# One PSUM pool of single banks, block sums on VectorE, and a new written order, in a memory-attention kernel with a spatial gate

## The chip, the cores and the metric

The kernel runs on one core of a Trainium2 chip. Times are device microseconds of one execution; lower is better. Runs of the same kernel are compared by their median. The profile is that of one execution, by the hardware profiler.

## The reference

Eight batches (B), eight heads (H), 576 positions (S), head dimension 64, 32 memory slots, inner width 1024.

```python
a   = softmax(phi over positions)                  # per batch and head
k_m = einsum('bhsm,bhsd->bhmd', a, k)              # memories: 32 x 64 per head
v_m = einsum('bhsm,bhsd->bhmd', a, v)
attn = softmax(q @ k_m.T / 8) ; x = heads joined of attn @ v_m   # (b, 576, 512)
h = relu(x @ w_in) ; u, v = h[..., :512], h[..., 512:]
v_n = (v - mean(v)) / sqrt(var(v) + 1e-6)          # over the 512 columns
v_s = einsum('ts,bsd->btd', w_spatial, v_n) + b_spatial[:, None]
out = (u * v_s) @ w_out
```

## The kernel before, in words

Everything is float32. Where precision asks for it an operand is split into a high part (rounded to `fp32r`) and a low part (the rest, by a subtraction), and a product is three matmuls: high by high, high by low, low by high. So most results on TensorE are groups of 3, 6 or 12 matmuls, and each operand costs one copy on ScalarE (`...h`) and one subtraction, mostly on VectorE (`...l`).

One batch goes through these Python generators; the letter is their name in the written order.

- `P` `memory_weights` (line 351): loads `phi`, takes its maximum over positions and the exponential; the sums over positions, `es`, run on VectorE for batches 0 to 2 and on POOL for the others (`over_rows`, line 340). Its scratch tile `half` shares the tag `o`, with two buffers, with the output tile `o` of line 962.
- `K` `memories` (389): loads `k` and `v` in two parts into one buffer, tag `kv`, and multiplies by the weights: the `kvm` matmuls (412), 80 for the first part and 64 for the second. The same tag `kv` holds `vraw`, the gate's values, for batches over 0; so a load waits until the batch before has read `vraw` for the last time (line 803), the second part waits for the first part's matmuls, and the next `vraw` for the second part's.
- `Q` `queries`, `S` `scores` (611): transposes, scores on TensorE, softmax on VectorE and ScalarE, then `ah` and `al`.
- `M` `products` (675): the memories' values times `w_in`, in a two-bank tile `mp`, split into `mh` and `ml`.
- `V` `gate` (703): for five tiles of positions (the fifth of 64 rows), v of the inner layer into one bank `pv`, ReLU on ScalarE into `vraw` (767), mean and variance by two VectorE instructions (770, 771), three small POOL instructions on 128x1 columns (773 to 777), and the normalisation on ScalarE (782). Batch 0 takes the statistics another way (754 to 765): ReLU with an accumulated sum, two small POOL instructions for the mean, a Square on ScalarE with the negative mean as bias and an accumulated sum.
- `A` `blend` (792): the spatial product of 576 by 576 is done as seven block products in place of eight. For it `vraw` is combined by four additions (809) and split into `vh` (801) and `vl` (803), seven each.
- `U` `units` (824): u for one of four column tiles, 12 matmuls into the two banks of `pu`, one ReLU of 576 columns on ScalarE (844).
- `G` `spatial` (849): the seven block products for one of two column pairs, 50 matmuls of 288 columns into two two-bank tiles: `pa` holds `c11` and `p6`, `pb` holds `c12` and `c21`. `c11`, `c12` and `c21` are used twice: a first product is read, and a second is then added to it in PSUM. ScalarE copies `c11` to `p1` (895), `c21` to `p7` (899), `c12` to `p5` (911); VectorE adds `p6` to `p1` (903); POOL adds `p7` and `p1` to `p5` (913, 915); the gated results are products into `u` (907 on VectorE; 917, 925, 929 on POOL) and are split into `gh` and `gl`.
- `O` `project` (945): 12 matmuls per tile of 128 positions into one bank `po`, a copy to `o` (963) and the store. The fifth tile is done once for two batches.

For the weights there are `D` and `E`/`L` (loading and decoding `w_in`), `X` (`w_out`), `W`, `T`, `B` and `Y` (the spatial weights), and `Z` (idle matmuls).

PSUM has eight banks. Before, four are a pool of single banks (`bank`, line 107) and four a pool of two tiles of two banks (`banks`, line 110), which `mp`, `pu`, `pa`, `pb` and the transposes of the spatial weights take.

The order is written out by hand. In the strings `START`, `PLAN` and `END` a letter, a number and a count say which generator goes one step on; a dash means a batch ahead. `PLAN` is used for each of the middle batches. A step issues what stands between two `yield`s, each engine works through its own instructions in that order, and engines wait for each other only where the data or a buffer asks for it (`manual_schedule`, line 1011). All DMAs are issued on SP's queue in the same order. `ON_VECTOR` names the operations that VectorE takes in place of POOL (or of TensorE and ScalarE, in `low`).

Of the kernel before, what the change touches and what calls it, by code (L numbers as in the profile page):

```python
# [20 lines left out]
    P*2 Q P*2 K P D1 Q*3 K Q K P K P Q P*2 Q P*2 D1 Q D0 Q*2 P*4 K Q E0 K P E0 Q E1 E0 Z P E0 W  # L21
    K Z K E1 K*2 Z K W E1 W Z P' Z K T4 K*2 L0 S E1 Z*4 K T3 B S B S*3 T3 S T0 X1 S D0 S T1 K' Z
    S*2 B*2 S T0 L0 S*2 Z*2 P' M1 S L1 Z*3 S L0 B P' T1 Q' M1 Z*2 M1 Z S*2 X1 M1 P' S*2 K' X1 Q'
    S X1 S M1 S M1 L0 P' S L1 T4 S P'*2 S T2 P' S Y L1 S T2 T4*2 X1 P' X1 V0 V1 P'*2 K' V0 L1 X0
    S X1 Y T4 P' V4 M0 Y K' V1 Y V1 Y P' V0 P'*2 Q' M0 X0 Y M0 Q' Y V0 T4 V4*2 T4*2 M0 Y K' M0 Y
    V2 T4 V2 M0 K' X0 K' Y*2 K' X0 U0 Q' M0 V0 U3 U0 Y K' Q' K' Y P'' K' P'' V1 V2 K' Y*2 K'*2
    P'' V3 Y Z X0 K' U3 S' U0 V1 V3 A*2 X0 V2 A S' U1 S' P'' V4 S'*2 X0 V3 V2 V4 V3 Z*2 V4 U3
    Z*2 A V3 Z S' A U2 A S' X3 A P'' V4 U2 P'' G0 V4 U2 V4 U1 A P'' A V4 A*2 G0 K'' A K'' Z G0 A
    Z U1 A S' P'' A G0 A*2 G0 X3 G0*2 P'' A X3 G0*3 G1 G0*2 P'' S' G0*5 P'' X3 K'' G1*2 G0 S' G0
    G1 G0 K'' S' G1*2 P'' G1 S' G1*3 M1' G0 G1 P'' G1 K''*2 G1 S' P''*2 G1 S' P''' M1' S'*2 G1  # L30
    X3 G1 S' K'' G1 X2 G1*2 M1' G0 S' M1'*2 M0' K'' X3 S' K'' M0' G1 M1' G0 V1' P''' M0' K'' X3
    G0*2 G1*2 K'' V0' G1 V1' G1 S' G1 V2' V3' U0' Q'' M0' V2' V1' V3' X2 P'''*2 X2 V1' M0' U0'
    K'' P''' V4' X2 V0' V4' V1' P''' V0' Q'' X2 U2' V2' V0' V2' P''' O0 K'' U2' P'''*2 V3' V0'
    X2 K''*2 V4' V2' A' P''' O3 X2 O2 V4' O2 A' V3' P''' A'*2 U0' V3' V4'*2 A' P'''*3 Q'' U2' O2
    V4' O2 A' V4' A' U1' V4'*2 A'*2 O1*2 A' Q'' O0 U3' P''' Q'' O3 U3' A'*2 U1' O1 U3' O0 Q''
    A'*2 O1 O3 K''' A' G0' S'' G0' O3 S'' U1' A' S'' A'*2 S'' K''' S'' G0'*7 G1' G0'*2 G1' G0'*3
    S''*2 G0'*2 S'' G0'*2 K''' O0 S''*2 G1' S''*2 G1'*2 S'' G1' G0' G1' G0'*2 G1' S'' G1'*2 G0'
    S''*2 M1'' S'' G0' S'' G0' M1'' S'' M1'' G1' S'' G0' M1''*2
# [3 lines left out]
    K'' G1 M0' P''' V1' V3' K'' V2' V4' V0' U2' U3' V0' V3' U2' K'' U3' K'' Q'' U0' V1' V4'*2  # L42
    U2' V0' Q'' S'' K'' V0' Q''' U1' V4' U3' U1' P''' U0' V3' S'' V4' P''' S'' A' V3' A' O2 V3'
    P''' A' S'' P''' V2' S'' U1' A' S'' A' V4' A'*2 P''' A' P''' O2 U0' A' S'' A' O3*2 V4' S''
    A' G0' V4' O0 G0'*2 A'*2 P''' A' G0' O2 G0' P''' S'' A' G0'*2 A' O1 G0' K''' G0' P''' A' G0'
    S'' A' G0'*2 S'' G0' O1 G0'*2 P''' K''' G1' G0'*2 S'' P''' O1 P''' O1 G0' P''' S'' O4*2
    G1'*2 S''*2 O4 G1' O2 S'' G1'*4 S'' Q''' G1'*4 K''' G0' S''*2 K'''*2 M1'' S'' O0 G1' M1''
    G1' P''' M1''*3 G1'*2 M0'' K'''*2 G1' Q''' O0*2 V2'' G0'*2 O3 G0' O3 K''' G1' V1'' M0'' G1'
    K''' V4'' G1' O4 V2'' M0'' K''' V2'' M0'' Q''' G1' G0'*2 V1'' G1' G0' V0'' G1' V4'' G1' V1''
# [15 lines left out]
)  # L65

# [4 lines left out]
def memory_attention_spatial_gate(  # L71
# [13 lines left out]
    nc = tc.nc  # L85
# [18 lines left out]
    ps1 = ctx.enter_context(tc.tile_pool(name="ps1", bufs=4, space=PSUM))  # L104
    ps2 = ctx.enter_context(tc.tile_pool(name="ps2", bufs=2, space=PSUM))
# [3 lines left out]

    def banks(name):  # L110
        return ps2.tile([P, 2, 512], F32, tag="b2", name=name)
# [121 lines left out]
    def transpose_spatial(b, si):  # L233
        w_sb, w_rem, _ = state["spatial"]
        if si == NI:

            w_dup = one.tile([P, NI, 2, SR], F32, tag="grh", name="w_dup")
            w_rem_dup = one.tile([SR, 2, SR], F32, tag="grl", name="w_rem_dup")
            nc.gpsimd.tensor_copy(w_dup, w_sb[:, :, None, SM:S].to_broadcast([P, NI, 2, SR]))
            nc.gpsimd.tensor_copy(w_rem_dup, w_rem[:, None, SM:S].to_broadcast([SR, 2, SR]))  # L240
            yield
        tp = banks(f"wt_{si}")
        for ti in range(NI + 1):
            if si < NI:
# [15 lines left out]
        x = tp.rearrange("p a s -> p (a s)")[:, 0:S]  # L260
        if si < NI:
            if "wraw" not in state:
                state["wraw"] = one.tile([P, 2, 4, HALF], F32, tag="vl", name="wraw")
            half, t = divmod(si, 2)
            nc.scalar.copy(
                state["wraw"][:, t, 2 * half : 2 * half + 2],
                x.rearrange("p (c s) -> p c s", c=2),
            )
            yield
            return  # L270
        nc.scalar.copy(ws1, x)
        yield
        diff = two.tile([P, HALF], F32, tag="p1", name="diff")
        nc.scalar.copy(diff, x[:, HALF:S])
        yield
        nc.vector.tensor_tensor(diff, x[:, 0:HALF], diff, op=ALU.subtract)
# [5 lines left out]
        yield from low(f"wtl{si}", ws2[0:SR], x[0:SR], ws1[0:SR])  # L282
# [392 lines left out]
    def products(b, f):  # L675
# [9 lines left out]
        both = banks(f"mp_{b}_{f}")  # L685
        mps = [both[:, r] for r in range(2)]
# [16 lines left out]
    def gate(b, st):  # L703
# [48 lines left out]
        if b == 0:  # L752

# [4 lines left out]
            squares = one.tile([P, DM], F32, tag="gh", name="squares")[0:rows]  # L758
# [16 lines left out]
        on_vector = f"norm{b}" in ON_VECTOR  # L775
# [48 lines left out]
    def units(b, dt):  # L824
# [4 lines left out]
        pu = banks(f"pu_{b}_{dt}")  # L829
        cs = slice(dt * P, (dt + 1) * P)  # L830
        n = 0
        for r in range(2):
            for m, a in ((mh, ah), (mh, al), (ml, ah)):
                for hf in range(2):
                    nc.tensor.matmul(  # L835
                        pu[:, hf, 0:HALF],
                        m[:, r, cs],
                        a[:, r, hf * HALF : (hf + 1) * HALF],
                        start=(n == 0),
                        stop=(n == 5),  # L840
                    )
                n += 1
            yield
        nc.scalar.activation(  # L844
            u[:, dt, :].rearrange("p (a s) -> p a s", a=2), pu[:, :, 0:HALF], AF.Relu
        )
        yield

    def spatial(b, x):
# [39 lines left out]

        p1 = two.tile([P, HALF], F32, name="p1")  # L890
# [12 lines left out]
        nc.vector.tensor_tensor(p1, p1, p6, op=ALU.add)  # L903
        yield
# [11 lines left out]
        yield  # L916
        engine("g22").tensor_tensor(g[:, x + 2, right], g[:, x + 2, right], p5, op=ALU.mult)
# [3 lines left out]
        product(c12, 6, 3, False, (0, ws1[:, right], ws2[:, right]))  # L921
        yield
        nc.vector.tensor_tensor(p7, p1, c21, op=ALU.add)
        yield
        engine("g21").tensor_tensor(g[:, x + 2, left], g[:, x + 2, left], p7, op=ALU.mult)
# [3 lines left out]
        engine("g12").tensor_tensor(g[:, x, right], g[:, x, right], p1, op=ALU.mult)  # L929
# [121 lines left out]
```

## Time and profile before

| what | us |
|---|---|
| median of 3 runs | 477.79 (474.4 to 478.72) |
| profiled execution | 476.24 |
| its span, first to last instruction | 474.5 |
| busy: TensorE / VectorE / ScalarE / POOL | 416.6 / 325.6 / 260.2 / 194.0 |
| mean granted TensorE clock | 0.96 |

The span leaves out 1.74 us of the execution's own time. TensorE's busy time counts overlapping matmuls by modelled ends, so a full stretch isn't one at peak; how fast matmuls follow each other is read from the chain.

### The profile page before, as it was taken

The page shows a single profiled execution, that of the slowest core. Times are in us where ns is not written, and L with a number is a line of the kernel's source. Part 1 is how long each engine was busy: PE and PEld are TensorE (multiplying, and loading weights), DVE is VectorE, ACT ScalarE, POOL GpSimd, SP SyncE. Part 2 cuts the span into 40 slices and gives each one's busy share as a digit, 9 for nine tenths or more (in the row PEclk, how much of TensorE's full clock was granted, in tenths as well). Part 3 has the DMA queues.
Part 4 walks back from the last instruction along what each step waited for, and adds up shares of the span by engine and source line. Part 5 has one row for each costly group of instructions (what it writes and reads, how often), then busy time and mean ns, then how long its engine had stood idle before and what let it go on. Part 6 is the DMA issues. An engine that isn't in the chain of part 4 may idle for free.

```text
span 474.5 us, 9479 instructions
## 1 busy us (share of the span) xinstructions
PE 416.6 (88%) x3781; PEld 335.9 (71%) x3781; DVE 325.6 (69%) x557; ACT 260.2 (55%) x506; POOL 194.0 (41%) x291
## 2 busy tenths in 40 slices
PE   3598797989888999899969999899979999998976
PEld 2474466767766878668757788768767888797855
DVE  2677999889579798369944997379935994564130
ACT  3446899267544764368423872467516862674131
POOL 1031682454444354425354445424445522564310
PEclk9858998999999999999988999999979999999989
DMA  8998414339145942864067133844085001200112
GB/s 302 382 306 133 135 51 155 92 96 99 46 155 149 93 50 63 153 197 53 0 178 162 54 47 112 161 140 52 3 196 142 1 1 46 68 1 1 44 66 90
DMA packets 94176, 50.70 MB, mean 107 GB/s; under 512 B 66418, under 2 KB 86898, under 8 KB 94132
## 3 DMA queue, kind: packets, MB, share of 16 engines
q1 hardware_dynamic: 94132, 50.10, 43.6%
q8 instruction: 30, 0.49, 0.5%
q14 instruction: 14, 0.11, 0.1%
HBM read 40.65 MB, written 9.44 MB: 106 GB/s over the span
## 4 chain that ended last, share of the span: by engine, by line
PE 42%; DVE 22%; POOL 9%; DMA 9%; ACT 8%; issue 7%; SPq 3%; POOLq 0%; DVEq 0%; ACTq 0%
PE po L957 8%; PE pb L881 7%; PE pa L881 6%; PE pu L835 5%; PE pv L725 5%; DVE vl L803 5%; DMA kv<-in_v_dram 4%; PE kvm L412 3%; DMA raw<-in_moe_w_in_dram 3%; DVE work L634 2%; POOL p L915 2%; DMA q_sb<-in_q_dram 1%; PE sc L621 1%; SPq L398 1%; PE mp L689 1%
## 5 line engine op out<-in xcount | busy, mean ns | idle before, releaser
L803 DVE TENSOR_TENSOR vl<-vraw,vh 128x512 fp32r<-128x512 f32 x56 | 48.3, 870 | 10.2 <-ACT vh L801 9.9
L957 PE MATMUL po<-woh,gh 128*128 128x512 f32 x128 | 52.3, 409 | 3.2 <-ACT gh L932 3.0
L809 POOL TENSOR_TENSOR vraw<-vraw 128x512 f32<-128x512 f32 x21 | 33.0, 1571 | 47.1 <-DVE vraw L809 32.1
L957 PE MATMUL po<-woh,gl 128*128 128x512 f32 x128 | 50.9, 397 | 0.0
L957 PE MATMUL po<-wol,gh 128*128 128x512 f32 x128 | 50.7, 396 | 0.0
L963 ACT COPY o<-po 128x512 f32<-128x512 f32 x36 | 21.1, 589 | 53.0 <-POOL es L346 27.4
L881 PE MATMUL pa<-bh,vh 128*128 128x288 f32 x96 | 31.7, 330 | 20.0 <-DVE p L903 12.2
L913 POOL TENSOR_TENSOR p<-p,p 128x288 f32<-128x288 f32 x16 | 12.9, 805 | 85.9 <-ACT p L911 85.9
L881 PE MATMUL pb<-bh,vh 128*128 128x288 f32 x128 | 39.4, 307 | 4.0 <-ACT u L844 2.1
L801 ACT CAST vh<-vraw 128x512 fp32r<-128x512 f32 x56 | 34.3, 619 | 13.4 <-DVE vraw L809 11.7
L881 PE MATMUL pb<-bl,vh 128*128 128x288 f32 x128 | 38.2, 299 | 0.0
L881 PE MATMUL pb<-bh,vl 128*128 128x288 f32 x128 | 38.1, 298 | 0.0
L881 PEld LDWEIGHTS pa<-bh,vh 128*128 128x128 f32 x96 | 18.7, 195 | 25.6 <-DVE p L903 15.0
L957 PEld LDWEIGHTS po<-woh,gh 128*128 128x128 f32 x128 | 24.5, 192 | 11.5 <-issue 4.2
L911 ACT COPY p<-pb 128x288 f32<-128x288 f32 x16 | 6.4, 400 | 46.1 <-PE pb L881 46.1
L835 PE MATMUL pu<-ah,mh 128*128 128x288 f32 x128 | 30.2, 318 | 0.9 <-ACT u L844 0.9
L881 PEld LDWEIGHTS pb<-bh,vh 128*128 128x128 f32 x128 | 24.6, 192 | 7.7 <-ACT u L844 3.4
L881 PE MATMUL pa<-bh,vl 128*128 128x288 f32 x96 | 29.2, 304 | 0.0
L881 PE MATMUL pa<-bl,vh 128*128 128x288 f32 x96 | 29.1, 303 | 0.0
L412 PE MATMUL kvm<-kv,phi_sb 64*32 64x128 f32 x1152 | 22.0, 291 | 8.0 <-DMA kv<-in_v_dram 6.5
L957 PEld LDWEIGHTS po<-woh,gl 128*128 128x128 f32 x128 | 24.3, 190 | 6.1 <-DVE gl L934 0.3
L412 PEld LDWEIGHTS kvm<-kv,phi_sb 64*32 64x32 f32 x1152 | 17.7, 112 | 15.1 <-issue 11.8
(209 smaller groups left out, 1232.7 us busy)
## 6 DMA issues: line engine op xcount, KB each, us to landing
out_dram<-o SPq DMA_DIRECT2D x32, 256.0 KB, 2.4
q_sb<-in_q_dram SPq DMA_DIRECT2D x28, 288.0 KB, 6.0
kv<-in_k_dram SPq DMA_DIRECT2D x8, 640.0 KB, 4.8
kv<-in_v_dram SPq DMA_DIRECT2D x8, 640.0 KB, 5.7
phi_sb<-in_phi_dram SPq DMA_DIRECT2D x8, 576.0 KB, 4.3
raw<-in_moe_w_in_dram SPq DMA_DIRECT2D x4, 1024.0 KB, 13.5
kv<-in_k_dram SPq DMA_DIRECT2D x8, 512.0 KB, 4.7
kv<-in_v_dram SPq DMA_DIRECT2D x8, 512.0 KB, 5.7
```

The source lines that it names most:

```text
L412: nc.tensor.matmul(kvb[r][32 * j : 32 * j + 32, 0 : 2 * D].rearrange("p (n d) -> p n d", n=2), phi_sb[halves[r], j, i, :], kv[halves[r], j ...
L634: nc.vector.transpose(sm[:, r, c].rearrange("p i m -> p (i m)"), sc[r][c][:, 0:HALF])
L725: nc.tensor.matmul(pv, x[:, r, cs], m[:, r, DM:DFF], start=(n == 0), stop=(n == 5))
L801: nc.scalar.copy(vh[:, :, to], raw[:, :, x])
L803: nc.vector.tensor_tensor(vl[:, :, to], raw[:, :, x], vh[:, :, to].bitcast(F32), op=ALU.subtract)
L809: engine(f"A{n}" if b else f"A{n}0").tensor_tensor(raw[:, :, to], raw[:, :, x], raw[:, :, y], op=op)
L835: nc.tensor.matmul(pu[:, hf, 0:HALF], m[:, r, cs], a[:, r, hf * HALF : (hf + 1) * HALF], start=(n == 0), stop=(n == 5),)
L881: nc.tensor.matmul(to, s_, m, start=first and n == 0, stop=n == len(ops) - 1, skip_group_check=True,)
L913: nc.gpsimd.tensor_tensor(p5, p5, p7, op=ALU.add)
L915: nc.gpsimd.tensor_tensor(p5, p5, p1, op=ALU.add)
L957: nc.tensor.matmul(po, a, w, start=(n == 0), stop=(n == 11))
L963: nc.scalar.copy(o, po)
```

## The change

PSUM becomes one pool of eight single banks. `products`, `units` and `transpose_spatial` take two tiles of it in place of a two-bank tile, with an evacuation each in `units` and `transpose_spatial` (there the last of the five goes through a tile in SBUF, and its low part is formed on VectorE). The blocks of `spatial` are four tiles taken where they are first needed; the copies of `c21` and `c12` and POOL's two adds are gone, and VectorE forms `p7 = p1 + c21` and `p5 = p7 + c12` from PSUM. The gate's statistics go for all batches the way of batch 0, and the Square is written into the PSUM bank that held the tile. `START`, `PLAN` and `END` are written anew (20 idle matmuls in place of 26). In `PLAN` the two column pairs of `spatial` are interleaved, the projection and most of the units stand between the gate and the block products, and both products and copy of `c11` stand well ahead of its continuation.

```diff
 PLAN = """
-    K'' G1 M0' P''' V1' V3' K'' V2' V4' V0' U2' U3' V0' V3' U2' K'' U3' K'' Q'' U0' V1' V4'*2
...
+    G1 M1' P'' G0 K'' G1 S' M1' K'' G1 G0*2 G1*3 S' G0 G1 K'' G1 M0' G0 G1 K''*2 M1'*2 M0' K''
...
+ON_SCALAR = set("st0 st1 st2 st3 st4".split())
...
-    ps1 = ctx.enter_context(tc.tile_pool(name="ps1", bufs=4, space=PSUM))
-    ps2 = ctx.enter_context(tc.tile_pool(name="ps2", bufs=2, space=PSUM))
+    ps1 = ctx.enter_context(tc.tile_pool(name="ps1", bufs=8, space=PSUM))
...
-        both = banks(f"mp_{b}_{f}")
-        mps = [both[:, r] for r in range(2)]
+        mps = [bank(f"mp_{b}_{f}_{r}") for r in range(2)]
...
-        if b == 0:
+        if b == 0 or f"st{st}" in ON_SCALAR:
             nc.scalar.activation(vr, pv, AF.Relu, accum_out=sums[:, 0:1])
...
-            squares = one.tile([P, DM], F32, tag="gh", name="squares")[0:rows]
+            squares = whole[0:rows]
...
-        pu = banks(f"pu_{b}_{dt}")
+        pu = [bank(f"pu_{b}_{dt}_{hf}")[:, 0:HALF] for hf in range(2)]
...
         for r in range(2):
-            for m, a in ((mh, ah), (mh, al), (ml, ah)):
-                for hf in range(2):
+            for hf in range(2):
+                for n, (m, a) in enumerate(((mh, ah), (mh, al), (ml, ah))):
...
-        nc.scalar.activation(
-            u[:, dt, :].rearrange("p (a s) -> p a s", a=2), pu[:, :, 0:HALF], AF.Relu
-        )
+        for hf in range(2):
...
+                nc.scalar.activation(u[:, dt, at[hf]], pu[hf], AF.Relu)
+            yield
...
-        one_, two_ = banks(f"pa_{b}_{x}"), banks(f"pb_{b}_{x}")
-        c11, p6, c12, c21 = (y[:, n, 0:HALF] for y in (one_, two_) for n in range(2))
...
+        c11 = block("pa")
         product(c11, 0, 0, True)
         yield
         nc.scalar.copy(p1, c11)
         yield
+        c21 = block("pc")
         product(c21, 1, 1, True, (1, ws1[:, right], ws2[:, right]))
         yield
-        nc.scalar.copy(p7, c21)
-        yield
+        p6 = block("pb")
         product(p6, 5, 5, True)
         yield
         nc.vector.tensor_tensor(p1, p1, p6, op=ALU.add)
         yield
+        nc.vector.tensor_tensor(p7, p1, c21, op=ALU.add)
+        yield
         product(c11, 2, 2, False, (0, ws1[:, left], ws2[:, left]))
         yield
         nc.vector.tensor_tensor(g[:, x, left], g[:, x, left], c11, op=ALU.mult)
         yield
+        c12 = block("pd")
         product(c12, 4, 4, True)
         yield
-        nc.scalar.copy(p5, c12)
-        yield
-        nc.gpsimd.tensor_tensor(p5, p5, p7, op=ALU.add)
-        yield
-        nc.gpsimd.tensor_tensor(p5, p5, p1, op=ALU.add)
-        yield
...
+        nc.vector.tensor_tensor(p5, p7, c12, op=ALU.add)
+        yield
...
         product(c21, 3, 6, False, (1, wd1, wd2))
         yield
+        nc.vector.tensor_tensor(p7, p1, c21, op=ALU.add)
+        yield
+        engine(f"g21{x}").tensor_tensor(g[:, x + 2, left], g[:, x + 2, left], p7, op=ALU.mult)
+        yield
         product(c12, 6, 3, False, (0, ws1[:, right], ws2[:, right]))
```

## Rows read from the trace of the kernel before

**Rows 1.** The page's first part: busy time of each engine, its share of the span, instructions.

```profile
PE 416.6 (88%) x3781; PEld 335.9 (71%) x3781; DVE 325.6 (69%) x557; ACT 260.2 (55%) x506; POOL 194.0 (41%) x291
```

**Rows 2.** The chain that ended last, in order of time (start us, us, what): the later half of the `kvm` matmuls of batches 3 to 7 (line 412).

```profile
149.46 0.93 PE kvm L412 x64
...
205.82 1.15 PE kvm L412 x63
...
259.22 1.08 PE kvm L412 x63
...
310.65 1.15 PE kvm L412 x63
...
363.15 1.15 PE kvm L412 x63
```

**Rows 3.** The same chain, seven of its pieces that are matmuls without a gap between them, for what each kind costs. `pa` and `pb` are the tiles of the block products, `po` of the projection, `pv` of the gate, `pu` of the units, `mp` of the products, `sc` of the scores; 80 is the number of matmuls of the first `kvm` half.

```profile
256.08 2.11 PE pb L881 x16
...
260.61 1.49 PE pv L725 x6
...
214.43 2.38 PE pu L835 x18
...
218.67 1.24 PE sc L621 x32
...
258.20 1.02 PE mp L689 x16
...
303.06 1.34 PE kvm L412 x80
...
112.03 1.39 PE po L957 x6
```

**Rows 4.** Busy time of each engine in two stretches of one batch period (stretch, its length, then each engine's busy us with its instructions, granted TensorE clock, DMA share, GB/s). 237.7 us is where the last `vl` of that batch ends.

```profile
205.80:237.70 31.90, 30.89 (x253) 25.51 (x254) 28.30 (x52) 22.52 (x45) 11.62 (x20) 1.00 0.29 55
...
237.70:259.20 21.50, 17.60 (x195) 14.43 (x198) 8.92 (x15) 6.73 (x13) 11.23 (x15) 0.84 0.74 179
```

**Rows 5.** Who waited for whom (engine, tile, line, releaser: us in total, times, longest us); the last row is the DMA queue's own.

```profile
PE pa L881 <- DVE p L903: 12.2, 15, 1.3
...
PE pa L881 <- ACT p L895: 5.5, 4, 2.3
...
ACT o L963 <- POOL es L346: 27.4, 5, 6.1
...
POOL few L773 <- DVE few L771: 41.0, 16, 5.0
...
SPq L398 <- DVE vl L803: 74.4, 5, 17.7
```

**Rows 6.** TensorE's instructions in order of time around 245 us, two that waited (idle time before, and what ended it, in brackets).

```profile
245.50 0.40 PE L881 MATMUL pa<-bh,vh 128*128 128x288 f32 x1 [2.32 <-ACT p L895]
...
247.59 0.61 PE L881 MATMUL pa<-bh,vh 128*128 128x288 f32 x1 [1.03 <-DVE p L903]
```

**Rows 7.** Busy time of each engine in the stretch behind these two waits (columns as in group 4).

```profile
246.00:254.00 8.00, 6.97 (x115) 6.05 (x113) 3.22 (x6) 1.29 (x4) 2.09 (x3) 0.57 0.94 141
```

**Rows 8.** The same columns for three whole batch periods and for the greater part of the head.

```profile
205.80:259.20 53.40, 48.49 (x446) 39.94 (x451) 37.22 (x66) 29.25 (x57) 22.85 (x34) 0.94 0.47 105
...
259.20:310.60 51.40, 48.31 (x454) 39.48 (x451) 38.54 (x68) 27.92 (x54) 23.83 (x35) 1.00 0.43 101
...
310.60:363.10 52.50, 48.06 (x439) 39.43 (x439) 37.41 (x66) 29.24 (x57) 22.89 (x34) 0.93 0.48 106
...
36.00:120.00 84.00, 72.67 (x705) 53.41 (x705) 75.97 (x124) 61.46 (x125) 41.22 (x61) 0.96 0.51 107
```

**Rows 9.** Groups of instructions by line (line, engine, operation, out<-in, shapes, count | busy us, mean ns of one | idle time before and what ended it). Lines 754 to 763 ran for batch 0 alone.

```profile
L770 DVE BATCH_NORM_STATS2 st<-vraw 128x6 f32<-128x512 f32 x28 | 19.1, 683 | 4.1 <-ACT vraw L767 4.1
...
L771 DVE BATCH_NORM_AGGREGATE few<-st 128x2 f32<-128x6 f32 (+1 forms) x35 | 6.3, 181 | 2.2
...
L759 ACT ACTIVATE squares<-vraw,few 128x512 f32<-128x512 f32 x4 | 2.9, 725 | 1.8 <-POOL few L756 1.8
...
L759 ACT ACTIVATION_READ_ACCUMULATOR squares<-vraw,few 128x1 f32 x4 | 0.8, 193 | 0.0
...
L756 POOL TENSOR_SCALAR few<-few 128x1 f32<-128x1 f32 (+1 forms) x5 | 1.7, 339 | 1.3 <-ACT vraw L754 1.3
...
L774 POOL TENSOR_TENSOR few<-few,half_neg 128x1 f32<-128x1 f32 (+1 forms) x40 | 25.6, 639 | 3.3
...
L844 ACT ACTIVATE u<-pu 128x576 f32<-128x576 f32 x32 | 20.5, 641 | 1.6 <-PE pu L835 1.5
...
L911 ACT COPY p<-pb 128x288 f32<-128x288 f32 x16 | 6.4, 400 | 46.1 <-PE pb L881 46.1
...
L913 POOL TENSOR_TENSOR p<-p,p 128x288 f32<-128x288 f32 x16 | 12.9, 805 | 85.9 <-ACT p L911 85.9
...
L915 POOL TENSOR_TENSOR p<-p,p 128x288 f32<-128x288 f32 x16 | 19.8, 1239 | 1.2
...
L923 DVE TENSOR_TENSOR p<-p,pb 128x288 f32<-128x288 f32 x16 | 7.3, 454 | 24.4 <-PE pb L881 20.8 <-POOL p L915 3.6
```

**Rows 10.** The DMA queue in order of time, one issue of a `kv` load; and the DMA issues by line (KB each, median us from issue to landing).

```profile
237.67 0.39 SPq L398 DMA_DIRECT2D kv<-in_k_dram  x1
...
kv<-in_v_dram SPq DMA_DIRECT2D x8, 640.0 KB, 5.7
```

More of the change, by code (lines that the diff above doesn't have):

```diff
@@ L26 @@
[L26 to L37, printed above, removed]
@@ L241, in transpose_spatial @@
             yield
-        tp = banks(f"wt_{si}")
+        tp, tr = bank(f"wt_{si}"), bank(f"wr_{si}")
         for ti in range(NI + 1):
@@ L264, in transpose_spatial @@
             half, t = divmod(si, 2)
-            nc.scalar.copy(
-                state["wraw"][:, t, 2 * half : 2 * half + 2],
-                x.rearrange("p (c s) -> p c s", c=2),
-            )
+            x = state["wraw"][:, t, 2 * half : 2 * half + 2].rearrange("p c s -> p (c s)")
+            nc.scalar.copy(x[:, 0:512], tp)
+            yield
+            nc.scalar.copy(x[:, 512:S], tr[:, 0:SR])
             yield
             return
-        nc.scalar.copy(ws1, x)
+        last = one.tile([P, S], F32, tag="u", name="last")
+        nc.scalar.copy(last[:, 0:512], tp)
+        yield
+        nc.scalar.copy(last[:, 512:S], tr[:, 0:SR])
+        yield
+        nc.scalar.copy(ws1, last)
         yield
         diff = two.tile([P, HALF], F32, tag="p1", name="diff")
-        nc.scalar.copy(diff, x[:, HALF:S])
-        yield
-        nc.vector.tensor_tensor(diff, x[:, 0:HALF], diff, op=ALU.subtract)
+        nc.vector.tensor_tensor(diff, last[:, 0:HALF], last[:, HALF:S], op=ALU.subtract)
         yield
@@ L281, in transpose_spatial @@
         yield
-        yield from low(f"wtl{si}", ws2[0:SR], x[0:SR], ws1[0:SR])
+        nc.vector.tensor_tensor(
+            ws2[0:SR], last[0:SR], ws1[0:SR].bitcast(F32), op=ALU.subtract
+        )
+        yield
     def blend_weights(b, _):
@@ L774, in gate @@
         nc.gpsimd.tensor_tensor(rs, rs, half_neg[0:rows], op=ALU.pow)
-        on_vector = f"norm{b}" in ON_VECTOR
+        on_vector = f"norm{st}" in ON_VECTOR and b > 0
         if not on_vector:
@@ L828, in units @@
         (ah, al, _), (mh, ml) = state["a", b], state["m", b]
[L829 removed]
         cs = slice(dt * P, (dt + 1) * P)
[L831 removed]
+        pu = [bank(f"pu_{b}_{dt}_{hf}")[:, 0:HALF] for hf in range(2)]
+        at = [slice(hf * HALF, (hf + 1) * HALF) for hf in range(2)]
         for r in range(2):
[L833 to L834 removed]
+            for hf in range(2):
+                for n, (m, a) in enumerate(((mh, ah), (mh, al), (ml, ah))):
                     nc.tensor.matmul(
[L836 removed]
+                        pu[hf],
                         m[:, r, cs],
[L838 to L840 removed]
+                        a[:, r, at[hf]],
+                        start=(r == 0 and n == 0),
+                        stop=(r == 1 and n == 2),
                     )
[L842 removed]
             yield
[L844 to L847 removed]
+        for hf in range(2):
+            if f"u{dt}{hf}" in ON_VECTOR:
+                nc.vector.tensor_scalar(u[:, dt, at[hf]], pu[hf], 0.0, None, op0=ALU.max)
+            else:
+                nc.scalar.activation(u[:, dt, at[hf]], pu[hf], AF.Relu)
+            yield
     def spatial(b, x):
@@ L888, in product, with block @@
                 )
+        def block(name):
+            return bank(f"{name}_{b}_{x}")[:, 0:HALF]
         p1 = two.tile([P, HALF], F32, name="p1")
@@ L920, in spatial @@
         yield
-        product(c12, 6, 3, False, (0, ws1[:, right], ws2[:, right]))
-        yield
         nc.vector.tensor_tensor(p7, p1, c21, op=ALU.add)
         yield
-        engine("g21").tensor_tensor(g[:, x + 2, left], g[:, x + 2, left], p7, op=ALU.mult)
+        engine(f"g21{x}").tensor_tensor(g[:, x + 2, left], g[:, x + 2, left], p7, op=ALU.mult)
+        yield
+        product(c12, 6, 3, False, (0, ws1[:, right], ws2[:, right]))
         yield
@@ L928, in spatial @@
         yield
-        engine("g12").tensor_tensor(g[:, x, right], g[:, x, right], p1, op=ALU.mult)
+        engine(f"g12{x}").tensor_tensor(g[:, x, right], g[:, x, right], p1, op=ALU.mult)
         yield
```

57 lines of the change are left out of this document (33 added, 24 removed).

## The prediction

> **What bounds the kernel now.** I read the shares of the engines first. TensorE is busy for 88% of the span and no other engine is over 69% [rows 1], so the question is how much of the span is TensorE's own work and how much is waiting that its modelled busy time hides.
>
> The second view is the chain that ended last. In it the second half of the `kvm` matmuls (63 or 64 of them) comes back once a batch: at 149.46, 205.82, 259.22, 310.65 and 363.15 us [rows 2]. The four periods between them are 56.4, 53.4, 51.4 and 52.5 us, 213.7 together. Ahead of them lies a head of 149.5 us, behind them a tail of 111.4.
>
> TensorE's own work in a batch follows from the same chain, where runs of matmuls without a gap are one piece [rows 3]. Block products: 100 matmuls, 16 in 2.11 us, 13.2. Projection: 4.5 tiles of 12, 6 in 1.39, 12.5. Gate: 28 matmuls, 6 in 1.49, 7.0. Units: 48, 18 in 2.38, 6.3. Memories: 1.34 and 1.15 [rows 2, 3]. Products: 32, 16 in 1.02, 2.0. Scores 1.24. Transposes and small ones some 0.7. Sum 45.4 us. So a period carries 6 to 8 us in which TensorE doesn't advance at full rate (the first one, with half a batch of projection more in it, somewhat less than its 11 us suggest).
>
> The stretches tell where. From 205.8 to 237.7 TensorE is busy 30.9 of 31.9 us, VectorE 28.3, ScalarE 22.5. From 237.7 to 259.2 TensorE is busy only 17.6 of 21.5 us, at a granted clock of 0.84 [rows 4]. The first stage is short of VectorE as well as of TensorE, and the second is where time is lost. The waits name the loss: the product that continues `c11` waits for the VectorE sum of line 903 in 15 of 16 cases, 12.2 us, and a product of the same tile waits 5.5 us for ScalarE's copy `p1` of line 895 [rows 5]. Neither is needed by the data in full: line 903 reads `p6`, which the continued product doesn't touch, and `p6` doesn't need the copy of `c11`. Both sit in one two-bank tile, `pa`, and the wait is for the tile. The wait for `p1` is long because ScalarE had stopped for `es` on POOL (27.4 us over five waits) [rows 5]. Around 245 us the two waits take 2.32 and 1.03 us [rows 6], and then the granted clock is down to the lower of its two levels, 1.2 GHz, for a while: 0.57 as a mean over 246 to 254 us [rows 7], which costs 0.43 x 8 = 3.4 us more.
>
> **The change, part by part**, against the profiled execution's own 476.24 us (span 474.5 and 1.74 around it); the median of the runs shown, 477.79, is 0.3% above it, and about 1% is what a measurement of this kernel can tell.
>
> *Single banks.* `c11`, `p6`, `c12` and `c21` become tiles of their own. `p6` no longer waits for `p1`, and the continued `c11` waits for the copy of `c11` alone, which in the new order stands several TensorE steps earlier. I count both waits as gone, 17.7 us over the whole run [rows 5], 2.2 a batch if spread evenly, 9 us in the four middle periods; the lower clock adds 3 to 4 us in two of these, where the mean is 0.94 and 0.93 [rows 8].
>
> *Sums on VectorE alone.* Per batch four copies leave ScalarE (0.40 each, 1.6), four adds leave POOL (0.81 and 1.24 twice, 4.1), and four VectorE additions from PSUM come (0.45 each, 1.8) [rows 9]. The continued `c21` now needs the first of them; `c11` continued and `c12` (14 matmuls, 1.9 us) stand between in the order, so I price that new wait at nothing; if VectorE comes to it late, it costs what the old wait did, 0.8 us a time.
>
> *Statistics of v.* Per batch VectorE loses 5 x (0.68 + 0.18) = 4.3 us. ScalarE gains a Square and two reads of the accumulator per tile, 0.73 + 2 x 0.19 = 1.1, so 5.6 us. POOL gains two small operations less one, about 0.4 to 0.7 a tile [rows 9]. The wait of POOL for VectorE's statistics (41.0 us) [rows 5] goes; a wait of ScalarE for POOL comes, since Square needs the mean from POOL. Behind it in ScalarE's queue are the next `relu`, the normalisations and `vh`. The new order puts another tile's `relu` or Square between in three of five cases.
>
> Square now writes into the PSUM bank. No row shows a Square into PSUM; the one into SBUF takes 0.73 us [rows 9], a plain copy of 288 columns 0.40, and I take 0.73. The Trainium skill (ScalarE: Activation LUTs, Step-by-step: what each stage is for) says that ScalarE reaches PSUM faster than SBUF, with the caveat "only useful if TensorE doesn't need most of PSUM". By the first half the Square would be a little cheaper; by the caveat the held bank would delay TensorE. By the written order the banks in use reach eight and more where the units meet the block products, so the caveat is the half that bears on this case; it is a rival below.
>
> *Units in two banks.* One ReLU of 576 columns (0.64) becomes two of 288 (0.40 each by the copy) [rows 9]: ScalarE +0.6 a batch, TensorE nothing.
>
> *Engine sums.* ScalarE per batch 28.8 (mean of the three last periods) [rows 8] + 5.6 - 1.6 + 0.6 = 33.4. VectorE 37.7 - 4.3 + 1.8 = 35.2. POOL falls or stays. Within the first stage VectorE falls from 28.3 to about 25 and ScalarE rises from 22.5 to some 27.5, while the new order moves projection and units there: TensorE has 32 us. So TensorE leads every engine in both stages.
>
> *The new period.* TensorE's 45.4, with the 2% that the steps lose at their hand-overs (the first stage's steps sum to 30.2 and were busy 30.9 [rows 4]), is 46.5. The `kv` loads can't start before the last `vl` has been read (SP waited 74.4 us for that) [rows 5]; from issue to landing they take 0.5 + 5.7 [rows 10]. After the issue the new order has about 5.5 us of TensorE work before the first half of `kvm` and 5.0 before the second, so 0.7 and 1.2 us of waiting, 1.9. For all hand-overs between ScalarE, POOL and VectorE I add 1.1. Sum 49.5; four periods 198.0 in place of 213.7: **-15.7 us**. Ends: TensorE alone, 4 x 46.5 = 186 (-28); 4 x 53 (-2).
>
> *Head.* From 36 to 120 us VectorE is busy 76 of 84 us [rows 8]: it bounds. The counts to the same `kvm` give it about 2 us less. The decoding of one `w_out` block stands earlier, while VectorE still has gaps, but its load stands ahead of `v` and the whole of `w_in`. I take **-2 us**, ends -6 and +5.
>
> *Tail.* The same 97 us of TensorE work, ScalarE with 7 us more; the end still goes through the last product, VectorE, POOL, ScalarE and five projections. **-1 us**, ends -5 and +4.
>
> Sum: 476.2 - 15.7 - 2 - 1 = **457.5 us**.
>
> **Rivals.** (a) *The wait moves on.* VectorE has still 35 us per batch, and in the order it comes to `p1 + p6` with blocks of `vl` and score work ahead of it. If half of the gain returns as waits for VectorE or ScalarE, the period is about 51.5: 468 us. For it: VectorE was the fuller of the two helpers in the first stage, and a wait of 2 to 3 us has been followed by the lower clock [rows 6, 7]. Against it: the sums above leave VectorE 3 to 5 us behind TensorE throughout.
>
> (b) *No gain.* The waits of `pa` are absorbed again by the next bound, the load of `kv` and the in-order queues, and what is left is within 1%: 476 us. For it: TensorE already fills 31 of 32 us in the first stage, so moving more work into it lengthens that stage.
>
> (c) *Slower: ScalarE's queue holds the banks.* Five Squares per batch each wait for POOL (up to 1.7 us by 0.34, 0.64 and the hand-overs [rows 9] where nothing else lies between), and the ReLUs of the units, which free banks, stand behind them. At the second bank of unit 0 the order gives TensorE 27.2 us of work since the `kvm` half and ScalarE 22.9; with all five round trips open ScalarE is at 31.4, TensorE waits 4.2 and then runs at the lower clock for 8 us (3.4): 7.6 per batch, over six batches 46 on the 457.5: 503. It decides from 3.1 us per batch on, where the whole 18.7 are gone; in its middle I put it at 488.
>
> (d) *Better.* The loads hide and TensorE alone bounds: 447 us.
>
> **Chances.** Forecast (450 to 463) 0.50, (a) 0.20, (b) 0.12, (c) 0.11, (d) 0.07. The range for 8 in 10 goes from 448, near TensorE alone, to 477, where (b) is half in. Against the median, faster by over 1% is under 473: forecast, (a) and (d), 0.77. Within 1%: 0.12. Slower: 0.11.
>
> **What would show it.** Right: no wait of the block products for the sum with `p6` or the copy `p1` worth a microsecond; halves of `kvm` 49 to 50 us apart; a granted clock of 1.00 through the middle; VectorE near 310 us in all (325.6 - 30 + 14.5) and ScalarE near 291 (260.2 + 39 - 13 + 5). Wrong: TensorE waiting for ScalarE's ReLU or Square (c), or for VectorE's new sums (a); waits of `kvm` for its load well over 2 us a batch; a head longer than 152 us.

## The result: 444 us in place of 478, below the range

Changed kernel: median 444.25 us (439.05 to 445.92), the kernel before beside it 478.25 (474.40 to 479.48). The ratio is 0.9266, 95% interval 0.916 to 0.937: faster by 7.3%, 34 us. The forecast was 457.5, its range 448 to 477. The profiled execution is the fastest of the four, 439.05 (span 437.1); against the profile before it is 37.4 us shorter in span, of which some 3 are that run's: it lies 5.2 under its kernel's median, the profile before 2.0 under its own. Its mean granted clock was 0.984, that of the other three 0.962 to 0.969.

The page's first part after, beside [rows 1]:

```profile
PE 397.1 (91%) x3773; PEld 325.7 (75%) x3773; DVE 301.1 (69%) x520; ACT 276.7 (63%) x615; POOL 185.9 (43%) x329
```

VectorE came out at 301 (forecast 310) and ScalarE at 277 (291): the work moved as said, and cost less than I had put down. The later `kvm` halves of batches 3 to 7 in the chain that ended last, beside [rows 2] (start us, us, what):

```profile
143.72 1.15 PE kvm L415 x63
...
192.39 1.15 PE kvm L415 x63
...
238.36 1.15 PE kvm L415 x63
...
287.60 1.16 PE kvm L415 x64
...
333.49 1.15 PE kvm L415 x63
```

The periods are 48.7, 46.0, 49.2 and 45.9 us, together 189.8 in place of 213.7. They alternate because the fifth projection tile (12 matmuls, 2.8 us) is done every second batch. So the head became 5.7 us shorter, the middle 23.9, the tail 7.7. The stretches between the halves and one for the tail, beside [rows 8] (stretch, length, busy us of TensorE, its weight loads, VectorE, ScalarE, POOL, granted clock, DMA share, GB/s):

```profile
192.30:238.30 46.00, 44.27 (x439) 37.27 (x439) 34.05 (x60) 30.76 (x70) 22.21 (x40) 1.00 0.52 113
238.30:287.50 49.20, 47.09 (x451) 39.58 (x451) 33.90 (x60) 31.34 (x71) 22.42 (x40) 1.00 0.54 113
...
334.60:437.10 102.50, 97.36 (x600) 83.12 (x597) 54.60 (x91) 59.58 (x135) 37.23 (x73) 1.00 0.13 39
```

In this execution the clock is at its higher level, 2.4 GHz, through the middle and the tail, where [rows 8] have 0.94 and 0.93 in two of the three periods. All that TensorE waited for from 145 to 335 us, beside [rows 5]:

```profile
PE kvm L415 <- DMA kv<-in_v_dram: 5.7, 5, 1.7
PE po L959 <- ACT pv L760: 0.8, 2, 0.5
PE kvm L415 <- DMA out_dram<-o: 0.6, 1, 0.6
```

No block product waits any more. And the Square of line 760, which now writes into PSUM (compare the one into SBUF, 725 ns, in [rows 9]):

```profile
L760 ACT ACTIVATE pv<-vraw,few 128x512 f32<-128x512 f32 x32 | 22.0, 687 | 2.4 <-POOL few L757 2.4
...
L760 ACT ACTIVATION_READ_ACCUMULATOR pv<-vraw,few 128x1 f32 x32 | 6.1, 190 | 0.0
```

### The profile page after: what moved, and what is told of

It reads as the page before. It is cut to its first block, busy times and chain, and to the rows that moved or that the text cites. A ratio compares the mean times of both kernels' runs of the same rounds, so it can differ in the third digit from the quotient of the medians.

```text
span 437.1 us, 9577 instructions
## 1 busy us (share of the span) xinstructions
PE 397.1 (91%) x3773; PEld 325.7 (75%) x3773; DVE 301.1 (69%) x520; ACT 276.7 (63%) x615; POOL 185.9 (43%) x329
## 4 chain that ended last, share of the span: by engine, by line
PE 51%; DMA 13%; DVE 12%; ACT 11%; POOL 7%; issue 4%; SPq 1%; POOLq 0%; DVEq 0%; ACTq 0%
PE po L959 17%; DMA kv<-in_v_dram 8%; PE pu L836 7%; PE pv L727 6%; PE pc L880 4%; DMA w_all<-in_moe_w_spatial_dram 3%; PE pd L880 3%; PE pa L880 3%; PE kvm L415 3%; DVE vl L804 3%; POOL few L775 2%; PE mp L691 2%; ACT pv L760 2%; POOL few L778 2%; DMA phi_sb<-in_phi_dram 2%
## 5 line engine op out<-in xcount | busy, mean ns | idle before, releaser
L836 PE MATMUL pu<-ah,ml 128*128 128x288 f32 x128 | 37.8, 295 | 0.2 <-ACT ml L155 0.2
L836 PE MATMUL pu<-al,mh 128*128 128x288 f32 x128 | 37.7, 294 | 0.0
L700 ACT CAST mh<-mp 128x512 fp32r<-128x512 f32 x32 | 18.5, 584 | 28.6 <-PE mp L691 28.6
L919 POOL TENSOR_TENSOR u<-u,p 128x288 f32<-128x288 f32 x16 | 16.9, 1056 | 36.6 <-DVE p L917 36.6
L848 ACT ACTIVATE u<-pu 128x288 f32<-128x288 f32 x64 | 24.0, 405 | 13.2 <-PE pu L836 13.2
L783 ACT ACTIVATE vraw<-vraw,few 128x512 f32<-128x512 f32 x32 | 26.1, 815 | 4.1 <-POOL few L778 3.9
L959 PEld LDWEIGHTS po<-wol,gh 128*128 128x128 f32 x128 | 24.1, 188 | 4.4
L775 POOL TENSOR_TENSOR few<-few,half_neg 128x1 f32<-128x1 f32 (+1 forms) x40 | 25.7, 642 | 3.3
L727 PE MATMUL pv<-mh,ah 128*128 128x512 f32 x64 | 25.8, 403 | 1.1 <-ACT pv L760 1.1
L936 DVE TENSOR_TENSOR gl<-u,gh 128x512 fp32r<-128x512 f32 x32 | 24.2, 763 | 3.3 <-ACT gh L934 3.0
```

The costliest lines, as they stand in the source:

```text
L727: nc.tensor.matmul(pv, x[:, r, cs], m[:, r, DM:DFF], start=(n == 0), stop=(n == 5))
L775: nc.gpsimd.tensor_tensor(rs, rs, half_neg[0:rows], op=ALU.pow)
L783: nc.scalar.activation(vr, vr, AF.Identity, bias=sh, scale=rs)
L836: nc.tensor.matmul(pu[hf], m[:, r, cs], a[:, r, at[hf]], start=(r == 0 and n == 0), stop=(r == 1 and n == 2),)
L848: nc.scalar.activation(u[:, dt, at[hf]], pu[hf], AF.Relu)
L936: nc.vector.tensor_tensor(gl[:, dt], g[:, dt, 0:SM], gh[:, dt].bitcast(F32), op=ALU.subtract)
```

## The experiments

Two theories at the start. Theory A: the parts did it, above all the single banks. Theory B: the written order did it. Every ratio is to the kernel before on the same chip.

**Single banks alone, old order.**

```diff
-    ps1 = ctx.enter_context(tc.tile_pool(name="ps1", bufs=4, space=PSUM))
-    ps2 = ctx.enter_context(tc.tile_pool(name="ps2", bufs=2, space=PSUM))
+    ps1 = ctx.enter_context(tc.tile_pool(name="ps1", bufs=8, space=PSUM))
...
-        one_, two_ = banks(f"pa_{b}_{x}"), banks(f"pb_{b}_{x}")
+        c11 = block("pa")
...
```

> The kernel before with single banks alone, in the old written order (two ReLUs per unit, transposes in two banks; copies, POOL adds and VectorE statistics as before). Theory A (the shared two-bank tile was the loss): both waits of the block products go, 17.7 us of waiting and part of the slow clock, so 12 to 20 us faster, 458 to 466. Theory B (the new order is the gain, the parts alone don't bring it): the next in-order wait takes the place, 0 to 6 us faster, 472 to 478.

Measured: 464.42, ratio 0.976 (0.972 to 0.980). A in size. But the middle hardly moved, 213.9 to 212.5; the tail fell from 110.2 to 103.1. What TensorE waited for in the middle, 148.5 to 361 us:

```profile
PE kvm L411 <- DMA kv<-in_v_dram: 11.3, 4, 2.9
PE pa L879 <- ACT p L894: 4.8, 2, 2.4
```

The wait for the sum with `p6` is gone (7.3 us of the 12.2 in [rows 5] lay in the middle), and the wait for the load of `kv` has grown from 1.4 to 11.3. All four of its waits are for the second load of a batch. By the DMA queue's rows this load starts 2 to 4 us sooner after the `kvm` of the batch before, but takes 7.1 to 8.3 us from its first issue to landing, in place of 5.3 to 6.1. It now stands right behind the load of the next queries (issued at 244.39 and 247.30 us in one period; before, 246.06 and 253.73); that this lengthens it is not shown. The wait for ScalarE's copy `p1` stays at 4.8 of 5.5 us: it now stands before the continued `c11`, which needs that copy.

**Sums on VectorE alone, two-bank tiles, old order.**

```diff
-        nc.scalar.copy(p7, c21)
...
+        nc.vector.tensor_tensor(p7, p1, c21, op=ALU.add)
...
-        nc.scalar.copy(p5, c12)
...
+        nc.vector.tensor_tensor(p5, p7, c12, op=ALU.add)
...
-        nc.gpsimd.tensor_tensor(p5, p5, p7, op=ALU.add)
-        nc.gpsimd.tensor_tensor(p5, p5, p1, op=ALU.add)
```

> The kernel before with the block sums on VectorE alone, in the old order and the old two-bank tiles (the steps of the removed copies and POOL adds stay as empty steps). Theory A: the wait for the tile stays and the long wait of POOL (86 us) was off the path, but POOL's own 4.1 us per batch stood ahead of the es that stopped ScalarE, so 2 to 8 us faster, 470 to 476. Theory B: the same or up to 4 us faster, since VectorE, full in the first stage, gets 1.8 us more per batch.

Measured: 478.08, ratio 1.003 (1.000 to 1.007): nothing, which theory B allowed. The block products still wait 13.3 us for the sum with `p6`, 16 times.

**Banks and statistics, then all three parts, old order.** The old order holds more `few` columns open at a time, so these two have five buffers for them.

```diff
-        if b == 0:
+        if True:
...
-            squares = one.tile([P, DM], F32, tag="gh", name="squares")[0:rows]
+            squares = whole[0:rows]
```

> The kernel before with single banks and with the statistics of v on ScalarE (and five buffers for the small columns), in the old order. Theory A: as with single banks alone, and VectorE's 4.3 us per batch less come on top where the first stage is short of it: 16 to 26 us faster, 452 to 462. Theory B: the statistics put ScalarE's Square in an order not written for it, TensorE waits for held banks: 0 to 8 us faster, 470 to 478, or slower.

> All three parts (single banks, sums on VectorE, statistics on ScalarE) in the old written order: what the new order is worth is the distance from here to the changed kernel. Theory A: at least two thirds of the gain, 448 to 456. Theory B: less than a third, 467 to 478.

Measured: 489.93, ratio 1.032 (1.027 to 1.036), and 488.35, ratio 1.026 (1.023 to 1.029): slower, so the three parts without the order lose 12 us. Theory B had "or slower" for the first of the two; for all three parts it is neither theory's number. TensorE's waits with all three, whole span:

```profile
PE pu L834 <- ACT pv L758: 14.4, 9, 2.6
PE kvm L412 <- DMA kv<-in_v_dram: 12.9, 8, 2.7
...
PE tv L460 <- ACT pv L758: 6.0, 6, 1.2
PE pa L880 <- ACT p L895: 3.8, 2, 2.0
```

The units wait for a bank that a Square in ScalarE's queue still holds. That is rival (c), which happens in the old order. No run put the Square into SBUF instead, so what the held bank costs apart from ScalarE's longer queue is not shown.

**Banks and sums, old order.** The edit is the first and second together.

> Single banks and the sums on VectorE, in the old order, statistics of v still on VectorE. Beside the new order without the statistics (455.4) it gives what the order alone is worth where ScalarE holds no bank with a Square. If the order's worth is to make room for the Square, this comes out at 453 to 458, no slower than the new order without it. If the order is worth something by itself, it stays at the 462 to 467 of the banks alone.

Measured: 460.46, ratio 0.967 (0.960 to 0.973): between the two numbers, 4 us under the banks alone (the intervals overlap).

**New order, statistics on VectorE again.**

```diff
-        if b == 0 or f"st{st}" in ON_SCALAR:
+        if b == 0:
```

> The changed kernel with the statistics of v back on VectorE (28 and 7 pairs of instructions, 4.3 us per batch), ScalarE without Square and accumulators, in the new order. Theory A (VectorE's load in the first stage matters): VectorE catches up with TensorE and the block products wait for it: 4 to 12 us slower than the changed kernel, 448 to 456. Theory B (the new order has room on every engine): within 3 us of it, 441 to 447.

Measured: 455.39, ratio 0.956 (0.951 to 0.961), 11 us over the changed kernel. Beside the one before, the order is worth 5 us where no Square holds a bank, about the least that can be told apart. The number is theory A's, its mechanism is not: no block product waits for VectorE from 145 to 335 us. What POOL and ScalarE waited for from 145 to 335 us, first here, then in the changed kernel:

```profile
ACT vraw L783 <- POOL few L778: 23.1, 14, 3.4
...
ACT vr L783 <- POOL few L778: 6.6, 4, 1.7
...
POOL few L774 <- DVE few L772: 54.6, 12, 6.8
```

```profile
ACT pv L760 <- POOL few L757: 5.0, 8, 0.9
ACT vr L783 <- POOL few L778: 4.0, 4, 1.0
ACT vraw L783 <- POOL few L778: 2.8, 6, 0.6
...
POOL few L757 <- ACT vraw L755: 24.1, 8, 5.4
```

With the statistics on VectorE they stand in its queue behind other work, among it the transposes of the next queries. POOL waits for them, and ScalarE's normalisation for POOL: 29.7 us, against 6.8. With them on ScalarE a wait of the Square for POOL comes, 5.0 us, so in sum ScalarE waits 18 us less for POOL at these places.

**New order, copies on ScalarE and adds on POOL again.**

```diff
-        nc.vector.tensor_tensor(p7, p1, c21, op=ALU.add)
+        nc.scalar.copy(p7, c21)
...
-        nc.vector.tensor_tensor(p5, p7, c12, op=ALU.add)
+        nc.scalar.copy(p5, c12)
+        nc.gpsimd.tensor_tensor(p5, p5, p7, op=ALU.add)
+        nc.gpsimd.tensor_tensor(p5, p5, p1, op=ALU.add)
```

> The changed kernel with the block sums as before: ScalarE copies c21 and c12, POOL adds twice, in the new order at the steps of the VectorE sums. Theory A: ScalarE's copies stand behind its other work, the continued c21 and c12 wait for them: 5 to 15 us slower than the changed kernel, 449 to 459. Theory B: within 3 us, 441 to 447.

Measured: 446.83, ratio 0.937 (0.931 to 0.943): 2.6 us over the changed kernel, not told apart from it.

**Is TensorE alone the bound now?** The projection without its low-part third (its output lacks that part):

```diff
-            for a, w in ((h_, woh), (h_, wol), (l_, woh)):
-                nc.tensor.matmul(po, a, w, start=(n == 0), stop=(n == 11))
+            for a, w in ((h_, woh), (h_, wol)):
+                nc.tensor.matmul(po, a, w, start=(n == 0), stop=(n == 7))
```

> The changed kernel without the third of the projection that multiplies the low part of the gated values (144 of 432 matmuls of 512 columns left out, 144 x 0.231 = 33 us of TensorE's own work); nothing else moves. If TensorE alone bounds the middle and the tail, the time falls by 24 to 33 us, to 411 to 420. If the ring of kv loads or ScalarE (33 us a batch) bounds too, it falls by less than 15 us, to 429 or more.

Measured: 438.49, ratio 0.917 (0.912 to 0.923). Of 33 us of TensorE work only 6 came back. In the middle (143 to 340 us) it waits instead:

```profile
PE kvm L415 <- DMA kv<-in_v_dram: 8.4, 6, 3.5
PE pu L836 <- ACT u L848: 8.3, 4, 2.1
```

and its granted clock is lower there (columns as in [rows 8]):

```profile
147.10:338.70 191.60, 174.64 (x1713) 146.38 (x1709) 137.21 (x241) 123.76 (x282) 90.30 (x161) 0.96 0.53 113
```

Half of the 33 us, 16.6, lies in these four periods. The waits grew by 10 us against the changed kernel, and a mean of 0.96 over 192 us, with the clock at its lower level for a while behind each of the four waits for the ReLU, is some 7 us more. I took what holds it for the ring of the `kv` buffer (gate, blend, load, `kvm`) and cut that. The next three tell whether it was.

**Ring kept (control), ring cut, ring cut and less TensorE work.** The low part of the gated results is formed in place and the projection takes the high part a second time in its stead (in the third it leaves that product out), which frees 8 KB; in the second and third `vraw` takes them. The outputs of the first two lack the low part and count a product of the high part twice.

```diff
-                one.tile([P, 2, 4, 256], F32, tag="kv" if b else "gl", name="vraw"),
+                one.tile([P, 2, 4, 256], F32, tag="gl", name="vraw"),
...
-            state["g", b] = tuple(
-                one.tile([P, NJ, SM], F32R, name=name) for name in ("gh", "gl")
-            )
+            state["g", b] = one.tile([P, NJ, SM], F32R, name="gh"), None
...
```

> Control for the next two: the changed kernel without the tile of the gated results' low part (8 KB a partition). VectorE forms the low part in place, the projection multiplies the high part twice, so its low part is missing from the output; the work on each engine is the same. Both theories: 441 to 447, as the changed kernel.

> As the control (the projection's low part missing from the output), and the freed 8 KB hold the gate's values, which so no longer share the buffer of the loads of k and v: the ring from the gate through blend and load to the next kvm is cut. If the ring alone sets the period, it falls by several microseconds: 415 to 430. If TensorE's own work is as long as the ring, only the waits of kvm for the load (5 us) and what follows them go: 436 to 443. If neither, no change.

> The ring cut as in the one before, and the projection's low-part third left out altogether (144 matmuls, some 33 us of TensorE, missing from the output). With the ring kept, leaving out that third took only 6 us (438.5). If ring and TensorE are two equal bounds, cutting both gives most of the 33 back: 405 to 418. If a third bound (ScalarE's or VectorE's queue in the written order) holds the period, it stays at 425 to 438.

Measured: 443.00 (0.933; 0.926 to 0.940), 446.41 (0.937; 0.929 to 0.944) and 435.24 (0.914; 0.907 to 0.921). Cutting the ring gives nothing, with TensorE's work whole or cut. So my ring theory fell for the way through `vraw`. The cut leaves a smaller ring: both loads of a batch still share one buffer, so the second waits for the first part's matmuls, and every wait of over 0.2 us for a load that is left in the middle of these two kernels is for that second load. No run took this one away. The chain of the last shows what holds it; in one period, from the later `kvm` half at 194.37 to the next at 240.41:

```profile
194.37 1.15 PE kvm L415 x63
...
211.58 1.26 POOL vraw L810
...
212.92 1.19 POOL few L764
...
214.18 1.11 POOL few L775
...
215.39 0.27 POOL few L778
...
215.68 0.02 ACT vr L783
...
216.40 0.40 ACT u L848
216.80 0.04 issue
216.84 2.15 PE pu L836 x9
...
232.47 1.35 PE kvm L415 x80
...
234.25 6.02 DMA kv<-in_v_dram
...
240.41 1.15 PE kvm L415 x63
```

The gate's statistics go between ScalarE and POOL for five tiles, the ReLU of unit 3 stands behind the last normalisation in ScalarE's queue, and TensorE needs its bank: 22.4 us from the `kvm` half. In the changed kernel the whole projection, 12.5 us, stands in that stretch and no unit waits, so shortening it uncovers the wait.

**Unit 3's ReLUs on VectorE**: in that kernel, in the complete changed one, and in the one with the ring kept and less TensorE work.

```diff
-    A10 A20 A30 A40 A2 Y1 Y2 lY11 lY22 lY2 lY1
+    A10 A20 A30 A40 A2 Y1 Y2 lY11 lY22 lY2 lY1 u30 u31
```

> The kernel with the ring cut and the projection's low-part third left out (435.2), with both ReLUs of unit 3 on VectorE in place of ScalarE, where they stand behind the normalisation of the fifth gate tile, which waits for POOL. If ScalarE's queue, which holds unit 3's banks, is the third bound, TensorE's wait of 2.1 us a batch for that ReLU goes and the lower clock behind it: 8 to 14 us less, 421 to 428. If it isn't, 432 to 438.

> The changed kernel, complete, with both ReLUs of unit 3 on VectorE. There TensorE waits for no ReLU, since the projection's 12.5 us stand in that stretch: if the three bounds are near each other and TensorE's own work is the last, no difference beyond the measurement, 440 to 447. If the wait for the bank, hidden in TensorE's modelled busy time, still costs something, 433 to 439.

> The changed kernel with unit 3's ReLUs on VectorE and the projection's low-part third left out (missing from the output), the ring of the load buffer kept. If the bank wait alone held the period after that third was left out (438.5), it falls as with the ring cut: 421 to 430. If the ring is a bound of its own, it stays at 434 to 440 while the one with the ring cut falls.

Measured: 434.97 (0.915; 0.909 to 0.920), 445.50 (0.935; 0.930 to 0.940) and 434.69 (0.912; 0.906 to 0.917). The second is as expected. In the other two the theory's numbers, 421 to 428 and 421 to 430, were missed (the first lies in its "if it isn't"): ScalarE's place was not the whole third bound. The waits of the first of them from 143 to 340 us:

```profile
PE kvm L415 <- DMA kv<-in_v_dram: 6.5, 5, 2.7
PE pu L836 <- DVE u L846: 4.5, 4, 1.4
PE pu L836 <- DVE cm L367: 3.8, 4, 1.0
```

The units wait as long as before in sum, 8.3 us, now for VectorE's queue: once for `u`, which comes behind `vl`, and once for a bank that `cm` (the largest `phi`) reads behind the softmax and `vl`. Which of the helpers' in-order queues would hold the period without TensorE is left open. What is shown is that none of the three edits (a third off the projection, the ring through `vraw` cut, unit 3's ReLUs off ScalarE), alone or together, gives more than 10 us.

No run beat the changed kernel with its whole computation.

## Why the prediction missed

The parts of the time in the profiles (us). The marks are the two small `kvm` matmuls right behind the later halves of batches 3 and 7, about 1.1 behind those in [rows 2].

| kernel | head | middle | tail |
|---|---|---|---|
| before | 150.3 | 213.9 | 110.2 |
| sums, old order | 152.5 | 214.7 | 110.6 |
| banks, old order | 148.5 | 212.5 | 103.1 |
| banks and sums, old order | 146.5 | 209.1 | 102.3 |
| all parts, old order | 151.2 | 222.0 | 112.9 |
| new order, statistics on VectorE | 150.4 | 198.6 | 103.5 |
| changed | 144.8 | 189.8 | 102.6 |
| changed, ring kept (control) | 147.0 | 190.6 | 102.4 |

*The bound and the waits: right.* TensorE's own 45.4 us is the base. The two waits of the block products are gone, the clock is at 1.00 through the middle (0.99 in the control), the statistics' cost on ScalarE stayed hidden.

*The period: mis-sized, and the first step that failed.* I put 49.5 = 45.4 + 1.1 (2% at the steps' hand-overs) + 1.9 (loads) + 1.1 (other hand-overs). Measured 47.45 = 45.4 + 1.8 (the waits shown, 7.1 over four) + 0.25. The wait for the loads was right. The 2.2 us of hand-overs came out as 0.25 (0.7 in the control, whose clock was 0.99 there). The same columns over the four periods, in the new order with the statistics on VectorE and in the changed kernel:

```profile
150.40:349.00 198.60, 186.02 (x1785) 154.33 (x1781) 148.21 (x281) 109.64 (x222) 79.22 (x123) 1.00 0.49 108
```

```profile
144.80:334.60 189.80, 182.70 (x1785) 154.33 (x1781) 136.63 (x240) 123.97 (x282) 89.82 (x161) 1.00 0.53 114
```

With the statistics on VectorE a period is 49.65 us: TensorE busy 46.5, waits for loads 1.8, other waits 1.4. That is my sum nearly term by term. So the hand-overs that I added are those of the kernel without its third part, and the statistics' move, which ended most of them, has no term in the period. It is worth 2.2 us a period, 8.8 in the middle. The 2% itself was read rightly in the old order [rows 4]. TensorE's waits from 205.8 to 237.7 us before:

```profile
PE pa L881 <- DVE p L903: 0.9, 1, 0.9
PE kvm L412 <- DMA kv<-in_v_dram: 0.7, 1, 0.7
```

The second of these ended at 205.82 us, so it lies ahead of the stretch. 31.9 us less the first is 31.0, for steps that sum to 30.2. What was wrong was to carry it over. In four periods the two allowances make 8 of the 18.4 us between the forecast and the profiled execution; the tail makes 6.7 and the head 3.5.

*The tail: the second.* Forecast -1, measured -7.7, and -7.1 with the banks alone. I priced the tail by its TensorE work and by ScalarE's 7 us more and did not apply to it what I had applied to the middle. Its block products had the same shared tile, and its last projection waited for them. TensorE's waits from 364.2 to 474.5 before:

```profile
PE po L957 <- ACT gh L932: 3.0, 1, 3.0
PE pa L881 <- DVE p L903: 1.8, 3, 0.6
PE pb L881 <- ACT u L844: 1.0, 1, 1.0
PE pa L881 <- ACT vh L801: 0.6, 1, 0.6
PE pb L881 <- ACT p L911: 0.5, 1, 0.5
```

and after, from 334.6 to 437.1:

```profile
PE po L959 <- ACT gh L934: 1.4, 1, 1.4
PE pd L880 <- DVE p L917: 0.2, 1, 0.2
```

6.9 us became 1.6, and the clock went from 0.98 to 1.00 over the stretch (2% of 103 is 2 us): together 7.3 of the 7.7.

*The head: open.* Forecast -2, here -5.5, but the control with the same order has -3.3 and the new order with statistics on VectorE 0. Between single profiles the head differs by as much as it may have gained. The head of the changed kernel and of the control:

```profile
0.00:144.80 144.80, 117.00 (x1397) 88.24 (x1397) 109.89 (x189) 93.13 (x198) 58.86 (x96) 0.95 0.68 174
```

```profile
0.00:147.00 147.00, 120.05 (x1396) 91.06 (x1396) 110.74 (x189) 93.20 (x198) 59.08 (x96) 0.92 0.67 171
```

The granted clock alone, 0.95 against 0.92 (3% of 145 us is 4), can make up the 2.2 us between them.

*Where the middle's gain came from: wrongly assigned.* The middle before:

```profile
150.30:364.20 213.90, 197.28 (x1818) 161.18 (x1812) 154.94 (x269) 115.73 (x225) 96.97 (x141) 0.97 0.51 106
```

It became 24.1 us shorter. TensorE's waits of 16.4 us became 7.1, and a mean clock of 0.97 became 1.00 (some 6 us). Some 3 us only moved: before, 16 block products and 16 matmuls of the products (3.1 us by [rows 3]) stood between the marks that now stand in the head and the tail. These, and not half a batch of projection, are 3 of the 5 us by which the first period is longer than the third: both have 60 projection matmuls. I counted the two waits of the block products as 9 us there, spread evenly, where the trace before has 12.8 (7.3 and 5.5), and I counted them and the clock to the banks. The banks alone gave 1.4 us there: the wait moved to the load of `kv`, as rival (b) has it. Banks and sums gave 4.8, the order another 10.5, and the statistics 8.8 more. Of the order's 10.5 the 3.1 are the moved work, and head and tail grew by 3.9 and 1.2; what it did bring there is a clock of 1.00 in place of 0.96. The statistics I had priced as a relief that VectorE did not need, since by busy time it was behind TensorE (35 us of a period). What they shorten is the way from the gate to the blend: 18 us less of ScalarE waiting for POOL. That this way gave the 8.8 us is read from the waits; no run changed it alone. A busy sum doesn't show that; the wait of POOL for VectorE in [rows 5], 41.0 us, did, and I dropped it as "goes".

*The rivals.* (c) is real and large, but in the old order: there the statistics cost 28 us (460.5 to 488.4), in the new one they bring 11. Its place and mechanism were nearly right (the units wait, mostly for the Squares' own banks); my reading that the new order left the banks short was not: no unit waits there. What I had not priced is that the projection, 12.5 us, stands just where ScalarE works through the gate. (d), "the loads hide and TensorE alone bounds", gave the nearest number, 447. That is luck: its mechanism isn't what was found, and 447 isn't the sum of its own terms (186 for four periods with -2 and -1 gives 445.5; likewise the period of 51.5 in (a) gives 465.5, not 468). The loads do not hide in full (1.6 us a period), and TensorE is not alone: 33 us less of its work gave 6, and with unit 3's ReLUs on VectorE, where the clock stayed at 1.00 through the middle, 10.

*The range.* Its low end, 448, was the middle's end (-28) without those that I had written down for head and tail. The three ends together (-28, -6, -5) reach 437. A range from the text's own ends would have held the result.

The Trainium skill (ScalarE: Activation LUTs, Step-by-step: what each stage is for) was weighed with both halves: PSUM nearer to ScalarE, and the caveat that TensorE may need the banks. The trace agrees with the first (687 ns for 32 Squares, against 725 for the four in batch 0 before: 5%). The second shows in the old order, 14.4 us of waits, and not in the new one.

## What to carry to other kernels

Price the parts of a change in the order in which they will run: here three parts lose 12 us in the old order and gain 34 in the new, since the order decides what work lies over a held bank. When a tile is shared for no reason of the data, apply the repair to every stage that uses it, the tail too. And give each part a term of its own in the sum: value a move off an engine by the wait that its result ends, not by that engine's busy share.

## What the runs showed that was not expected

- In the changed kernel TensorE loses next to nothing at hand-overs: 0.25 us of a period of 47.45 is neither its own work nor a wait that the trace names. With the statistics on VectorE it was 1.1 of 49.65.
- In the kernels with less TensorE work the granted clock was lower. Without the projection's third the mean clock over the span was 0.943, with the ring kept and with it cut, against 0.984 in the changed kernel's profile and 0.969 in the control's. With unit 3's ReLUs on VectorE it was 0.963 and 0.968; the units' waits were as long in sum there, but none longer than 1.4 us, where they had been 2.1.
- The head took 144.8 and 147.0 us in two kernels whose order and work are the same, at a granted clock of 0.95 and 0.92.
